# A decayed-attention and gated-MLP kernel on one core: factors of chunk 1 loaded on their own, 128-row chunk loads, a head-by-head state update, and a re-planned order

## The chip, the core and the metric

The kernel runs on one core of one Trainium2 chip. The core's engines run side by side and meet only at semaphores: PE (TensorE, matrix products into the accumulators of PSUM), DVE (VectorE) and ACT (ScalarE) for elementwise work, POOL (GpSimd), and SP (SyncE), which in this kernel issues every transfer. TensorE's clock has two levels, 1.2 and 2.4 GHz; the profile shows the granted clock as a share of the higher one. The metric is device time in microseconds (us), the median over runs.

## The reference

For 4 batches of 8 heads, 768 steps and head width 48, a state of 48x48 per head is decayed row by row and fed with an outer product; the rows that come out, 8 heads side by side, go through a gated MLP.

```python
# q, k, v, alpha: (B=4, H=8, S=768, D=48); alpha in 0.8 .. 1.0
for t in range(S):
    state = alpha[:, :, t, :, None] * state + np.einsum('bhd,bhe->bhde', k[:, :, t], v[:, :, t])
    y[:, :, t] = np.einsum('bhd,bhde->bhe', q[:, :, t], state)
x = y.transpose(0, 2, 1, 3).reshape(B * S, H * D)      # 3072 x 384
h = x @ w_in                                           # w_in 384 x 2048
g = h * np.tanh(softplus(h))
out = g @ w_out                                        # w_out 2048 x 384
```

## The kernel before

**Chunks.** Time is cut into 6 chunks of 128 steps per batch, 24 chunks in all (numbered 0 to 23; number n is batch n % 4, so chunks 0 to 3 start from an empty state). A chunk's q, k and alpha lie in one tile `qka` of 112 rows: head pairs with one head's 48 features on rows 0 to 47, the other's on rows 64 to 111. Two such tiles exist, so the load of chunk n+2 waits until chunk n has been read for the last time. `attention(n)` makes these steps:

- DVE: two running products of alpha over the chunk, backwards (`scan_rest`, L492) and forwards (`scan_front`, L509), with a small reciprocal between them (L497); the factors are multiplied into k in two halves (L504) and into q (L519); an older state is decayed (L524).
- PE: the scores (L539, 16 products recorded as 32 matmuls), DVE's causal masks (L549, two), the output of the chunk (L594; 16 products for chunks 0 to 3, with 8 more for the state part after that).
- The output goes into the tile `xs` as a rounded high part and a low part (L611, then L616 on DVE, or L623 on PE and L631 on ACT for chunks 0 to 7); six small transfers (L637) put the last two heads' rows in their places.
- For all but the last chunk of a batch: a transpose of k on PE (`turn`, L702), a copy by ACT (L706), the update `k^T v` on PE (L711: one product per head pair, 112 by 96, of which only the two 48x48 blocks on the diagonal are wanted), and its addition to the state, one DVE instruction per head of a pair (L723; for chunks 0 to 3 ACT copies, L721).

**The MLP.** A unit is one block of 128 hidden columns (16 blocks, f) over 2 or 4 chunks (256 or 512 tokens): 9 matmuls of the first layer (L754: 3 slices of 128 features, each high x high, high x low and low x high), ACT's exponential and three more activations, DVE's three steps (L772, L781, L788), and 3 matmuls of 384 columns per chunk for the second layer (L816). There are 20 units of 2 chunks, then 86 of 4. The weights come as 64-bit words; DVE makes 32-bit numbers of them (L364, L369, L374, once for each of the two matrices), ACT rounds the high part (L379), and the low part comes from PE and ACT for blocks 0 to 3 (L403, L404, L407) and from DVE for the others (L393).

**The order.** A planner in the kernel (`Plan.order`) writes all engines' instructions out in advance. Each task has an engine, a cost, a time after which its result can be used, a key, and the buffers it uses. At each step the task that can begin first is put next on its engine, the one of lower key among equals, as the planner reckons. Where PE would stand idle the planner puts in filler matmuls (L866) that write to a free accumulator and whose result is not used. Each engine then works in its order, and an instruction that waits holds up all behind it. Keys: a chunk is due some units before its first unit, spaced at least 2 units apart; weights, loads and checks hang on the same scale.

Of the kernel before, what the change touches and what calls it, by code (L numbers as in the profile page):

```python
# [9 lines left out]
F32 = mybir.dt.float32  # L10
F32R = mybir.dt.float32r
# [4 lines left out]
ALU = mybir.AluOpType  # L16
# [11 lines left out]
B, H, S, D = 4, 8, 768, 48  # L28
# [9 lines left out]
QKA = (3 * C + 1) * NPAIR + 1  # L38

# [22 lines left out]
COLD = 16  # L62
FILL_BANKS = ("o3", "o2", "o1", "o0", "h", "att")
FILL_FROM, FILL_UNTIL = 2.4, 130.0
FILL_MARGIN = 0.1
EARLY_BANKS = {
    0: "o2 h o3 o0 att att".split(),
    1: "att att att att o3 att".split(),
    2: "o0 h h h att o1".split(),
    3: "o3 h att o1 att o0".split(),  # L70
    4: "att att att att o1 h".split(),
    5: "o2 o3 att o2 o2 att".split(),
}
X_PE = 8
W_PE = 4
W_DVE = 4
# [4 lines left out]
BEGIN = {"PE": 2.4, "DVE": 4.3, "ACT": 2.2, "POOL": 4.2, "SP": 1.2}  # L81
# [17 lines left out]
class Plan:  # L99
# [23 lines left out]
    def order(self):  # L123
# [8 lines left out]
        done, n, port_free = [], len(self.tasks), 0.0  # L132

# [39 lines left out]
        while len(done) < n + fills:  # L173
            best = None
            for e in ENGINES:
                first = None
                for t in waiting[e][:WINDOW]:
# [24 lines left out]
            free[e] = at + t.cost  # L202
            if t.port:
                port_free = at + t.cost
# [14 lines left out]
WINDOW = 150  # L219

COST = {
    "load part": (0.7, 3.3), "load q": (1.8, 5.0), "load v": (0.7, 4.0), "load w": (2.0, 5.0),
    "move": (0.63, 2.5), "store": (0.47, 3.0),
    "cold fill": (0.321, 0.36), "fill": (0.1635, 0.2), "off": (0.2, 0.35), "w off": (0.95, 1.2), "lead": (0.27, 0.38), "bits": (0.47, 0.58), "w hi": (0.42, 0.56), "w lo": (0.95, 1.08),
# [3 lines left out]
    "scores": (1.07, 1.08), "y0": (1.08, 1.1), "y": (1.7, 1.7), "turn": (0.4, 0.64),  # L228
    "turned": (0.43, 0.57), "update": (0.76, 0.98),
# [14 lines left out]
def fast_path(ctx, tc, qka, v, w, out, good):  # L244
# [57 lines left out]
    xs = [const.tile([P, 2, NPAIR, k * C], F32R, name=f"xs{i}") for i, k in enumerate(X_TILES)]  # L302
# [40 lines left out]
    def weight(f):  # L343
        key = weight_unit[f] - W_LEAD
# [9 lines left out]
        got = add("SP", *COST["load w"], max(key, FIRST_W + f) - 4, load, uses=[stage])  # L354
        fs = slice(f * P, (f + 1) * P)
        for m in range(2):
# [29 lines left out]
            k = key + 0.5 * m  # L386
# [29 lines left out]
    def weight_check(f):  # L416
        key = CHECK_FROM + f * CHECK_STEP
# [30 lines left out]
    def attention(n):  # L448
# [3 lines left out]
        st, key = state[b], due[n]  # L452
# [4 lines left out]
        Q = lambda: by_pair(q_buf.tile[:, : NPAIR * C])  # L457
        K = lambda: by_pair(q_buf.tile[:, NPAIR * C : 2 * NPAIR * C])
        alpha = lambda: q_buf.tile[:, 2 * NPAIR * C :]
# [680 lines left out]
```

## Time and profile before

| | us |
|---|---|
| median of 3 runs | 523.48 (521.75 to 523.56) |
| the profiled execution | 526.62 |
| its span, first to last instruction | 524.9 |
| PE busy in the span | 513.0 (98%) |
| DVE / ACT busy | 382.3 (73%) / 397.3 (76%) |
| second layer L816 / first layer L754 on PE | 227.4 / 217.8 |

The profiled execution took 1.7 us more than its span, and 3.1 us more than the median of the runs. A busy PE is not a PE at its peak: matmuls are pipelined and their ends are modelled, so work on PE is better read from one task's start to the next one's. DVE's 73% is a mean over stages that differ: until about 143 us the weights are being made beside the first ten chunks, after that they are not.

### The profile page before, as it was taken

The page shows a single profiled execution, that of the slowest core. Times are in us where ns is not written, and L with a number is a line of the kernel's source. Part 1 is how long each engine was busy: PE and PEld are TensorE (multiplying, and loading weights), DVE is VectorE, ACT ScalarE, POOL GpSimd, SP SyncE. Part 2 cuts the span into 40 slices and gives each one's busy share as a digit, 9 for nine tenths or more (in the row PEclk, how much of TensorE's full clock was granted, in tenths as well). Part 3 has the DMA queues.
Part 4 walks back from the last instruction along what each step waited for, and adds up shares of the span by engine and source line. Part 5 has one row for each costly group of instructions (what it writes and reads, how often), then busy time and mean ns, then how long its engine had stood idle before and what let it go on. Part 6 is the DMA issues. An engine that isn't in the chain of part 4 may idle for free.

```text
span 524.9 us, 11178 instructions
## 1 busy us (share of the span) xinstructions
PE 513.0 (98%) x4287; PEld 447.7 (85%) x4287; DVE 382.3 (73%) x743; ACT 397.3 (76%) x914; POOL 4.6 (1%) x34
## 2 busy tenths in 40 slices
PE   6999999999999999899999999999999999999996
PEld 4678989998898888788899888899988899999996
DVE  6899999999976876868777566886468654554452
ACT  1578789999699987888867856577776567787774
POOL 2000000000000000000000000000000000000000
PEclk9799999999999999999999999999999999999999
DMA  8656636413254866465320132220042000010001
GB/s 269 179 172 195 200 82 205 166 61 116 68 177 139 233 229 191 169 204 162 112 76 0 47 92 76 76 76 1 1 136 78 9 9 2 15 46 1 1 1 65
DMA packets 21818, 54.31 MB, mean 103 GB/s; under 512 B 4000, under 2 KB 14752, under 8 KB 21760
## 3 DMA queue, kind: packets, MB, share of 16 engines
q1 hardware_dynamic: 21760, 53.55, 33.2%
q8 instruction: 35, 0.57, 0.5%
q14 instruction: 23, 0.19, 0.1%
HBM read 46.45 MB, written 4.72 MB: 97 GB/s over the span
## 4 chain that ended last, share of the span: by engine, by line
PE 79%; DMA 8%; DVE 7%; SPq 3%; issue 2%; ACT 2%; DVEq 0%; ACTq 0%
PE bank L816 33%; PE bank L754 32%; DMA qka<-in_qka_dram 8%; PE bank L594 5%; PE bank L539 3%; SPq L637 2%; PE bank L711 2%; PE bank L702 1%; PE bank L403 1%; DVE rest L492 1%; DVE qka L509 1%; DVE t L781 1%; DVE y L772 1%; DVE g L788 1%; DVE xs L616 1%
## 5 line engine op out<-in xcount | busy, mean ns | idle before, releaser
L816 PE MATMUL bank<-wo,g 128*128 128x384 f32 x1152 | 227.4, 341 | 0.2 <-DVE part L843 0.2
L754 PE MATMUL bank<-xs,wi 128*128 128x512 f32 (+1 forms) x954 | 217.8, 373 | 1.8 <-DVE y L772 1.8
L816 PEld LDWEIGHTS bank<-wo,g 128*128 128x128 f32 x1152 | 198.3, 188 | 7.6 <-DVE part L843 0.4
L754 PEld LDWEIGHTS bank<-xs,wi 128*128 128x128 f32 x954 | 167.4, 188 | 28.9 <-DVE y L772 2.1
L762 ACT ACTIVATE u<-bank 128x512 f32<-128x512 f32 (+1 forms) x106 | 58.9, 555 | 82.7 <-PE bank L754 82.4
L772 DVE SCALAR_TENSOR_TENSOR y<-u,bank 128x512 f32<-128x512 f32 (+1 forms) x106 | 66.8, 631 | 49.2 <-ACT u L762 48.8
L788 DVE TENSOR_TENSOR g<-t,g 128x512 fp32r<-128x512 f32 (+1 forms) x106 | 67.2, 635 | 48.0 <-ACT g L785 47.8
L775 ACT ACTIVATE t<-t,tenth 128x512 f32<-128x512 f32 (+1 forms) x106 | 72.0, 679 | 2.3
L781 DVE SCALAR_TENSOR_TENSOR t<-y,t 128x512 f32<-128x512 f32 (+1 forms) x106 | 67.0, 633 | 5.1 <-ACT t L778 4.3
L768 ACT ACTIVATE t<-u 128x512 f32<-128x512 f32 (+1 forms) x106 | 62.6, 590 | 3.7 <-DVE g L788 1.4
L785 ACT ACTIVATE g<-t 128x512 fp32r<-128x512 f32 (+1 forms) x106 | 61.5, 581 | 5.1 <-DVE t L781 3.2
L778 ACT ACTIVATE t<-t 128x512 f32<-128x512 f32 (+1 forms) x106 | 61.6, 581 | 0.5
L492 DVE TENSOR_TENSOR_SCAN rest<-qka,behind 112x516 f32<-112x516 f32 x24 | 29.5, 1228 | 15.2 <-DMA qka<-in_qka_dram 15.2
L509 DVE TENSOR_TENSOR_SCAN qka<-qka,ahead 112x516 f32<-112x516 f32 x24 | 29.4, 1223 | 0.0
L549 DVE COPY_PREDICATED probs<-causal,bank 128x384 f32<-128x384 uint32 x48 | 25.8, 584 | 4.4 <-PE bank L539 4.1
L594 PEld LDWEIGHTS bank<-probs,v 128*64 128x64 f32 (+3 forms) x768 | 20.6, 128 | 8.5 <-issue 3.9
L594 PE MATMUL bank<-probs,v 128*64 128x64 f32 (+3 forms) x768 | 25.5, 227 | 1.5 <-DVE ahead L497 1.5
L539 PEld LDWEIGHTS bank<-qka 48*64 48x64 f32 x768 | 18.6, 137 | 5.8 <-issue 3.7
L539 PE MATMUL bank<-qka 48*64 48x64 f32 (+1 forms) x768 | 22.3, 255 | 0.0
L762 ACT ACTIVATION_READ_ACCUMULATOR u<-bank 128x1 f32 x106 | 20.7, 195 | 0.0
L611 ACT ACTIVATE xs<-bank 112x256 fp32r<-112x256 f32 x48 | 16.3, 373 | 5.6 <-PE bank L594 5.6
L711 PEld LDWEIGHTS bank<-v,ks 128*112 128x112 f32 x160 | 18.0, 177 | 1.8 <-ACT xs L631 0.5
(79 smaller groups left out, 348.4 us busy)
## 6 DMA issues: line engine op xcount, KB each, us to landing
qka<-in_qka_dram SPq DMA_DIRECT2D x23, 674.2 KB, 5.5
ws<-in_wp_dram SPq DMA_DIRECT2D x16, 768.0 KB, 4.6
wc<-in_wp_dram SPq DMA_DIRECT2D x16, 768.0 KB, 5.1
v<-in_vp_dram SPq DMA_DIRECT2D x24, 192.0 KB, 4.6
out_dram<-osb SPq DMA_DIRECT2D x16, 192.0 KB, 1.8
xs<-xs SPq DMA_DIRECT2D x144, 16.0 KB, 2.5
out_dram<-part SPq DMA_DIRECT2D x8, 192.0 KB, 3.1
qka<-in_qka_dram SPq DMA_DIRECT2D x2, 224.0 KB, 3.7
```

Source lines behind the costliest of these rows:

```text
L539: nc.tensor.matmul(p[a][to, i, blocks], K()[r : r + D, j, to], q.rearrange("p (x t) -> p x t", t=HALF), start=True, stop=True,)
L594: made = nc.tensor.matmul(o, l, r, start=begins, stop=m >= len(ops) - 2, skip_group_check=True)
L754: nc.tensor.matmul(p[:, :N], wi[:, z, s, fs], x[:, a, s], start=m == 0, stop=m == len(passes) - 1)
L762: nc.scalar.activation(wide(u), wide(h), AF.Exp, scale=-1.0, accum_out=uchk[:, at : at + 1])
L768: nc.scalar.activation(wide(t), wide(u), AF.Square, bias=1.0, scale=2.0)
L772: nc.vector.scalar_tensor_tensor(wide(y), wide(u), 0.5, wide(h), ALU.add, ALU.mult)
L775: nc.scalar.activation(wide(t), wide(t), AF.Ln, bias=tenth, scale=0.1)
L778: nc.scalar.activation(wide(t), wide(t), AF.Exp, scale=-1.0)
L781: nc.vector.scalar_tensor_tensor(wide(t), wide(y), 0.4, wide(t), ALU.mult, ALU.mult)
L785: nc.scalar.activation(g.tile[:, 0, :N], wide(t), AF.Copy)
L788: late[mybir.EngineType.DVE] = nc.vector.tensor_tensor(g.tile[:, 1, :N], wide(t), g.tile[:, 0, :N].bitcast(F32), ALU.subtract)
L816: made = nc.tensor.matmul(o.tile[:, :DM], g.tile[:, a, j * C : (j + 1) * C], wo[:, z, f], start=begins and m == 0, stop=end and m == 2,)
```

## The change

Seven things change together.

- Chunk 1's tile is loaded in two parts: alpha straight after chunk 0's three parts and ahead of chunk 0's v, then q and k.
- Chunks are laid out and loaded with 128 rows in place of 112, each row starting 6656 bytes after the last (6164 before); the 16 added rows are not computed with.
- The tile `xs` holds high and low part of a chunk side by side, so a small transfer moves 16 rows of 1024 bytes in place of 16 times two runs of 512; the first layer's moving operand, which was one run of 512 columns, is now four runs of 128 with gaps of the same size.
- The update makes one product per head, with 64 or 48 columns of the array and 48 moving columns, whose results lie on the same rows as the state, so that one instruction gathers them.
- Weight block 3's low part goes from PE and ACT to DVE (`W_PE`, `W_DVE` from 4 to 3).
- The planner knows of a queue of at most 8 transfers that move one after the other, and other costs; fewer first fillers count as cold (14).
- Keys of single chunks, units and weights are shifted by a table, and the banks of the early chunks are other ones.

```diff
-COLD = 16
+COLD = 14
+SHIFT = {
+    "chunk": {
+        4: -2, 5: -2, 7: 2.79, 21: -1,
+    },
+    "unit": {
+        0: -6, 1: -4, 2: -5, 3: -3, 4: -4.5, 7: -1, 9: -1, 25: 0.5, 27: -0.9, 31: 1.5, 32: 1.01,
...
+    },
...
+}
-W_PE = 4
-W_DVE = 4
+W_PE = 3
+W_DVE = 3
...
+                    if e == "SP" and len(landed) >= QUEUE:
+                        r = max(r, landed[-QUEUE])
...
+            if e == "SP":
+                moving = max(moving, at + DMA_FIRST) + t.late
+                landed.append(moving + DMA_LAST)
+                t.late = moving + DMA_LAST - at
...
+QUEUE = 8
+DMA_FIRST, DMA_LAST = 1.67, 0.3
...
-    xs = [const.tile([P, 2, NPAIR, k * C], F32R, name=f"xs{i}") for i, k in enumerate(X_TILES)]
+    xs = [const.tile([P, NPAIR, k, 2, C], F32R, name=f"xs{i}") for i, k in enumerate(X_TILES)]
...
-            t = new(q_buf, [R, QKA], f"qka{n}")
-            nc.sync.dma_start(t, qka[b, c])
+            t = new(q_buf, [P, QKA], f"qka{n}")
+            nc.sync.dma_start(t, qka[b, c, :, :QKA])
...
+        elif n == 1:
+            got_a = add("SP", *COST["load part"], -98.7, load_part(2 * NPAIR * C, QKA), uses=[q_buf])
+            got_k = got_q = add("SP", *COST["load qk"], -98.5, load_part(0, 2 * NPAIR * C), uses=[q_buf])
...
-                    x[48 + r : 64 + r, :, s, tok].bitcast(F32),
-                    x[r + 16 * s : r + 16 * s + 16, :, NK, tok].bitcast(F32),
+                    x[48 + r : 64 + r, s, place].bitcast(F32),
+                    x[r + 16 * s : r + 16 * s + 16, NK, place].bitcast(F32),
...
-                nc.tensor.matmul(
-                    p[:R, j, : 2 * D], ks_buf.tile[:, j], V()[:, 2 * D * j : 2 * D * (j + 1)],
-                    start=True, stop=True,
-                )
+                for a, wide in ((0, HALF), (1, D)):
+                    h = (2 * j + a) * D
+                    nc.tensor.matmul(
+                        p[64 * a : 64 * a + wide, j, :D], ks_buf.tile[:, j, 64 * a : 64 * a + wide],
+                        V()[:, h : h + D], start=True, stop=True,
+                    )
...
-                    p[:, :N], wi[:, z, s, fs], x[:, a, s], start=m == 0, stop=m == len(passes) - 1
+                    p[:, :N], wi[:, z, s, fs], x[:, s, :, a], start=m == 0,
+                    stop=m == len(passes) - 1,
...
-    qka = np.zeros((B, NCH, R, QKA), inputs["q"].dtype)
+    qka = np.zeros((B, NCH, P, QKA_ROW), inputs["q"].dtype)
```

What stands on SP at the start of the program, before: chunk 0's alpha, then its k and q, chunk 0's v, then chunk 1 whole (`qka_128`), its v, weight blocks 0 and 1 (`ws`), chunk 2 (`qka_218`).

```order
L470 DMA qka_116<-in_qka_dram 112x517
L470 DMA qka_116<-in_qka_dram 112x512 x2
L474 DMA v_124<-in_vp_dram 128x384
L465 DMA qka_128<-in_qka_dram 112x1541
L474 DMA v_139<-in_vp_dram 128x384
L349 DMA ws_145<-in_wp_dram 128x1536
L349 DMA ws_179<-in_wp_dram 128x1536
L465 DMA qka_218<-in_qka_dram 112x1541
```

The same place on SP now; chunk 1's tile is `qka_120`, chunk 2's `qka_254`, and `xs` rows are the small transfers of chunk 0's output.

```order
L498 DMA qka_116<-in_qka_dram 128x517
L498 DMA qka_116<-in_qka_dram 128x512 x2
L498 DMA qka_120<-in_qka_dram 128x517
L502 DMA v_124<-in_vp_dram 128x384
L498 DMA qka_120<-in_qka_dram 128x1024
L377 DMA ws_130<-in_wp_dram 128x1536
L502 DMA v_135<-in_vp_dram 128x384
L377 DMA ws_139<-in_wp_dram 128x1536
L667 DMA xs_111<-xs_111 16x256
L493 DMA qka_254<-in_qka_dram 128x1541
```

Chunk 1's alpha is now fourth and its q and k sixth; chunk 2's load stands behind one small transfer of chunk 0's output.

What stands on DVE after chunk 1's q product (L519), before: the masks of chunk 1 (`probs`), the last step of weight block 0, and then chunk 2's backward product (L492 on `qka_218`; this listing names running products SCALAR_TENSOR_TENSOR) with block 1's steps behind it.

```order
L374 SCALAR_TENSOR_TENSOR w_lead_0_235<-ws_145,w_lead_0_235 128x384
L549 COPY_PREDICATED probs_93<-causal,bank 128x384
L549 COPY_PREDICATED probs_95<-causal,bank 128x384
L374 SCALAR_TENSOR_TENSOR w_lead_1_238<-ws_145,w_lead_1_238 128x384
L492 SCALAR_TENSOR_TENSOR rest_301<-qka_218,behind 112x516
L364 TENSOR_SCALAR w_lead_0_310<-ws_179 128x384
L497 RECIPROCAL ahead<-rest_301 112x4
```

The same place on DVE now, with chunk 2's product at L523 on `qka_254` and block 1's words in `ws_139`.

```order
L402 SCALAR_TENSOR_TENSOR w_lead_1_231<-ws_130,w_lead_1_231 128x384
L580 COPY_PREDICATED probs_93<-causal,bank 128x384
L580 COPY_PREDICATED probs_95<-causal,bank 128x384
L392 TENSOR_SCALAR w_lead_0_304<-ws_139 128x384
L397 SCALAR_TENSOR_TENSOR w_lead_0_304<-ws_139,w_lead_0_304 128x384
L402 SCALAR_TENSOR_TENSOR w_lead_0_304<-ws_139,w_lead_0_304 128x384
L392 TENSOR_SCALAR w_lead_1_321<-ws_139 128x384
L523 SCALAR_TENSOR_TENSOR rest_327<-qka_254,behind 112x516
```

Weight block 0 is finished before chunk 1's masks, and four steps of block 1 now stand ahead of chunk 2's backward product.

What stands on PE for chunk 1's update now (before, one row, `L711 MATMUL bank<-v_139,ks_262 112x96 x4`), with the low part of weight block 1 (L431, L432) ahead of it and the first of 13 fillers behind it.

```order
L431 MATMUL bank<-w_lead_0_304,ident 128x384
L432 MATMUL bank<-wi,minus_ident 128x384
L743 MATMUL bank<-v_135,ks_283 64x48
L743 MATMUL bank<-v_135,ks_283 48x48
L743 MATMUL bank<-v_135,ks_283 64x48
L743 MATMUL bank<-v_135,ks_283 48x48
L743 MATMUL bank<-v_135,ks_283 64x48
L743 MATMUL bank<-v_135,ks_283 48x48
L743 MATMUL bank<-v_135,ks_283 64x48
L743 MATMUL bank<-v_135,ks_283 48x48
L895 LDWEIGHTS behind
L895 MATMUL bank<-behind 128x384
```

Four products of 96 moving columns have become eight of 48. Over the whole of PE's order there are now 50 fillers (43 before), 6 pairs of weight subtractions L431 and L432 (8 before), and the first unit's first layer stands after chunk 2's output and ahead of chunk 3's scores (before: behind chunk 3's scores).

## Rows read from the trace of the kernel before

**Rows 1.** The page: busy us, share of the span, instructions of each engine.

```profile
PE 513.0 (98%) x4287; PEld 447.7 (85%) x4287; DVE 382.3 (73%) x743; ACT 397.3 (76%) x914; POOL 4.6 (1%) x34
```

**Rows 2.** Windows: stretch, length, busy us (instructions) per engine, PE clock, DMA share, GB/s.

```profile
117.00:130.00 13.00, 13.00 (x84) 11.60 (x87) 13.00 (x29) 12.00 (x27) 0.00 (x0) 1.00 0.27 79
...
208.00:260.00 52.00, 49.90 (x464) 42.47 (x463) 38.96 (x72) 45.37 (x103) 0.26 (x3) 1.00 0.54 170
```

**Rows 3.** Finer windows of the start, the same columns.

```profile
2.50:7.50 5.00, 4.92 (x18) 2.49 (x19) 3.88 (x8) 0.46 (x2) 0.99 (x5) 1.00 1.01 281
...
19.00:20.00 1.00, 1.00 (x4) 0.68 (x3) 0.87 (x1) 0.28 (x1) 0.00 (x0) 0.50 0.13 31
```

**Rows 4.** Timeline of the start: start, busy, engine, line, tiles, shapes, [idle before <-releaser].

```profile
9.93 1.23 DVE L492 TENSOR_TENSOR_SCAN rest<-qka,behind 112x516 f32<-112x516 f32 x1 [2.23 <-DMA qka<-in_qka_dram]
11.08 1.02 DVE L549 COPY_PREDICATED probs<-causal,bank 128x384 f32<-128x384 uint32 x2
...
12.15 1.06 PE L594 MATMUL bank<-probs,v 128*64 128x64 f32 x32 [1.53 <-DVE ahead L497]
...
20.70 1.06 PE L594 MATMUL bank<-probs,v 128*64 128x64 f32 x32
...
24.98 0.90 PE L539 MATMUL bank<-qka 48*64 48x128 f32 x32
```

**Rows 5.** DMA issues from 0 to 4.2 us: count, KB each, median us to landing.

```profile
qka<-in_qka_dram SPq DMA_DIRECT2D x1, 674.2 KB, 7.2
```

**Rows 6.** Timeline of DVE, 26 to 47 us.

```profile
35.15 1.22 DVE L492 TENSOR_TENSOR_SCAN rest<-qka,behind 112x516 f32<-112x516 f32 x1
...
39.20 0.35 DVE L524 TENSOR_TENSOR state<-state,rest 112x192 f32<-112x192 f32 x1
...
40.44 0.62 DVE L364 TENSOR_SCALAR w_lead<-ws 128x384 int32<-128x384 int32 x2
...
42.85 1.05 DVE L549 COPY_PREDICATED probs<-causal,bank 128x384 f32<-128x384 uint32 x2
43.80 0.41 DVE L781 SCALAR_TENSOR_TENSOR t<-y,t 128x256 f32<-128x256 f32 x1
```

**Rows 7.** Timeline of PE, 26 to 47 us.

```profile
30.93 0.81 PE L403 MATMUL bank<-w_lead,ident 128*128 128x384 f32 x2
...
31.84 0.90 PE L539 MATMUL bank<-qka 48*64 48x128 f32 x32
...
39.70 0.90 PE L539 MATMUL bank<-qka 48*64 48x128 f32 x32
...
44.46 0.66 PE L594 MATMUL bank<-qka,state 48*48 48x128 f32 x16
```

**Rows 8.** Timeline of PE at a state update, 174 to 179 us.

```profile
176.69 0.93 PE L711 MATMUL bank<-v,ks 128*112 128x96 f32 x8
177.40 1.29 PE L816 MATMUL bank<-wo,g 128*128 128x384 f32 x6
```

**Rows 9.** Windows of L594 alone, PE and weight loads: middle part of a chunk's output.

```profile
302.82:303.43 0.61, 0.61 (x20) 0.54 (x16) 1.00 0.01 3
```

**Rows 10.** Groups by line and form: xcount | busy us, mean ns | idle before.

```profile
L723 DVE TENSOR_TENSOR state<-bank,state 48x192 f32<-48x192 f32 x32 | 11.3, 352 | 5.9 <-PE bank L711 5.7
```

**Rows 11.** The chain that ended last: start us, us, what.

```profile
85.72 1.08 PE bank L754 x9
...
109.36 2.08 PE bank L754 x9
111.43 2.08 PE bank L816 x12
```

**Rows 12.** Who waited for whom, DVE, 143 to 330 us: total us, times, longest.

```profile
DVE rest L492 <- DMA qka<-in_qka_dram: 11.8, 9, 3.6
```

**Rows 13.** The page: DMA issues over the span, median us to landing.

```profile
qka<-in_qka_dram SPq DMA_DIRECT2D x23, 674.2 KB, 5.5
ws<-in_wp_dram SPq DMA_DIRECT2D x16, 768.0 KB, 4.6
```

More of the change, by code (lines that the diff above doesn't have):

```diff
@@ L219 @@
 WINDOW = 150
+QUEUE = 8
+DMA_FIRST, DMA_LAST = 1.67, 0.3
 COST = {
-    "load part": (0.7, 3.3), "load q": (1.8, 5.0), "load v": (0.7, 4.0), "load w": (2.0, 5.0),
-    "move": (0.63, 2.5), "store": (0.47, 3.0),
-    "cold fill": (0.321, 0.36), "fill": (0.1635, 0.2), "off": (0.2, 0.35), "w off": (0.95, 1.2), "lead": (0.27, 0.38), "bits": (0.47, 0.58), "w hi": (0.42, 0.56), "w lo": (0.95, 1.08),
+    "load part": (0.47, 1.1), "load qk": (0.47, 1.8), "load q": (0.47, 2.7),
+    "load v": (0.47, 0.82), "load w": (0.45, 2.51), "move": (0.6, 0.15), "store": (0.47, 0.75),
+    "cold fill": (0.321, 0.36), "fill": (0.1635, 0.2), "off": (0.125, 0.3), "w off": (0.95, 1.2), "lead": (0.27, 0.38), "bits": (0.47, 0.58), "w hi": (0.42, 0.56), "w lo": (0.95, 1.08),
     "w check": (0.92, 1.2),
@@ L227 @@
     "state": (0.365, 0.4), "state0": (0.31, 0.35), "mask": (0.49, 0.63),
-    "scores": (1.07, 1.08), "y0": (1.08, 1.1), "y": (1.7, 1.7), "turn": (0.4, 0.64),
-    "turned": (0.43, 0.57), "update": (0.76, 0.98),
+    "scores": (1.02, 1.05), "y0": (1.1, 1.2), "y": (1.77, 1.79), "turn": (0.42, 0.64),
+    "turned": (0.43, 0.57), "update": (0.7, 0.9),
     "x hi": (0.275, 0.415), "x lo": (0.34, 0.455),
@@ L343, in weight @@
     def weight(f):
-        key = weight_unit[f] - W_LEAD
+        key, shift = weight_unit[f] - W_LEAD, SHIFT["weight"].get(f, 0.0)
         stage = plan.buffer("stage")
@@ L463, in load @@
         def load():
-            t = new(q_buf, [R, QKA], f"qka{n}")
-            nc.sync.dma_start(t, qka[b, c])
+            t = new(q_buf, [P, QKA], f"qka{n}")
+            nc.sync.dma_start(t, qka[b, c, :, :QKA])
         def load_part(lo, hi):
             def part():
-                t = q_buf.tile if q_buf.tile is not None else new(q_buf, [R, QKA], f"qka{n}")
+                t = q_buf.tile if q_buf.tile is not None else new(q_buf, [P, QKA], f"qka{n}")
                 nc.sync.dma_start(t[:, lo:hi], qka[b, c, :, lo:hi])
@@ L731, in attention @@
                 *(("ACT", *COST["state0"]) if first else ("DVE", *COST["state"])), key + 1.0,
-                gather(a, r), [t_u, t_y, *t_decay], [u_buf],
+                gather, [t_u, t_y, *t_decay], [u_buf],
             )
-            for a, r in enumerate((0, 64))
         ]
@@ L740, in unit @@
     def unit(c0, nt, f, at, ends):
-        N, key = nt * C, float(at)
+        N, key = nt * C, at + SHIFT["unit"].get(at, 0.0)
         tile_at, place = X_AT[c0]
-        x = xs[tile_at][:, :, :, place * C : place * C + N]
+        x = xs[tile_at][:, :, place : place + nt]
         fs = slice(f * P, (f + 1) * P)
```

64 lines of the change are left out of this document (35 added, 29 removed), and 2 rows, old and new, of the table SHIFT.

## The prediction

> **What bounds the kernel now.** I read the page first: PE is busy 98% of the span, DVE 73% [rows 1]. Then windows. From 30 us on PE hardly stands still: at 117 to 130 us it is busy all 13.00 us, and so is DVE [rows 2], so for the first ten chunks two engines are full at once. The steady pace is 2.08 us for a first layer of 512 columns and 2.08 for its 12 second-layer matmuls, start to start [rows 11], and 86 such units (with 20 of half the size) make some 400 us that the change leaves alone. Time can come only from work taken off PE, from the start, where PE runs fillers and waits for DVE, and from the idle 2.1 us (52.00 less 49.90) between 208 and 260 us [rows 2].
>
> At the start the chain goes through DVE. DVE waits 2.23 us until chunk 1's load lands and begins its backward product at 9.93; behind it the masks of chunk 0 come at 11.08 and PE's first output at 12.15, after 1.53 us with nothing to do [rows 4]. The granted clock then is at 0.50, the 1.2 GHz level, at 19 to 20 us [rows 3], and chunk 1's output, which stands behind weight block 0 on PE, comes at 20.70 [rows 4]. The first products of the MLP follow chunk 3's scores at 31.84 [rows 7].
>
> **Part by part.** All sums are made against the profiled execution, 526.62 us (span 524.9 and 1.7 around it). It lies 3.1 above the median of 523.48; I apply the same difference to the median.
>
> *Chunk 1's alpha first.* It is fourth in the queue: 1.05 MB with what stands ahead. At the 281 GB/s of 2.5 to 7.5 us [rows 3] that is 3.7 us of transfer, so it lands at about 6 us if transfers go strictly in order, and no later than 8 if those behind take a share (chunk 1's whole tile took 7.2 us from issue [rows 5]). I take 7.9, near the moment at which DVE is through with chunk 0. That takes 2.0 us off the wait, and its cover is gone at once: from there DVE is late by its own work. I follow it in the new order with start-to-start times: a chunk's backward and forward products and its three multiplications 3.7 us (35.15 to 39.20, less one unit step of 0.3), the six steps of a weight block 2.4 (40.44 to 42.85), two masks 0.95 (42.85 to 43.80) [rows 6]; the first product of a chunk is 1.2 of the 3.7.
>
> - product of chunk 1 at 7.9, masks of chunk 0 to 10.1: output 0 at 10.1 (before 12.15).
> - rest of chunk 1's factors 2.5, weight block 0 2.4, masks 0.95: output 1 at 16.0 (before 20.70).
> - four steps of block 1, 1.5. Chunk 2's load now stands behind the transposes of chunk 1, at about 13; with 5.5 us [rows 13] it lands at 18.7, and DVE waits 1.2 us for it, a new wait. Factors 3.7 and one weight step 0.5: scores of chunk 2 at 22.9 (before 24.98).
> - one weight step, product of chunk 3, masks: 25.5; rest of its factors 2.5: scores of chunk 3 at 28.0 (before 31.84).
> - three weight or unit steps and masks, 2.8; five small ones, 2.0; chunk 4's factors with two unit steps 4.3: scores of chunk 4 at 37.1 (before 39.70). Seven more steps, 3.0: output 4 at 40.2 (before 44.46).
>
> The lead is 4.3 us at output 4. DVE never strings its work together so tightly, and q and k of chunk 1 land with 1.78 MB, a little late; I take 3.5, with 1.0 (the alpha alone, half given back to the new wait) and 5.0 as ends. At that point PE also has more behind it: six second-layer matmuls more, 1.04 [rows 11], and one weight subtraction more, 0.9 (30.93 to 31.84 [rows 7]), but chunk 4's transposes and update not yet, 1.1 (the update 0.71 [rows 8], the transposes put at half of it). That is 0.9 in its favour: 4.4.
>
> *Update by heads.* Before, 0.71 us from the update's start to the next task (176.69 to 177.40 [rows 8]). After, eight products of 48 columns, two at a time on halves of the array. The nearest row is the middle part of a chunk's output: eight products of 64 columns with the same 128 rows and the same halves, 0.61 us with the change-over to that part (16 weight loads, two to a product) [rows 9]. By columns that is 0.46, by count of products 0.61; whether the 0.15 between them is a change-over or a price per product no row tells. I take 0.5, so 0.2 saved. The ends are 0 (the price per product and a change-over of 0.1 to 0.15 more) and 0.3. For chunks 4 to 19, where PE is full, 16 times 0.2 is 3.2; the four early updates lie beside DVE's chain and bring nothing.
>
> The section Key Properties of the Trainium skill's page "TensorEngine Tiling (Array Packing)" speaks against this part: a change of tiling mode drains the engine, and the update now enters and leaves a mode of half-width tiles. The trace has that 0.15 at one such change and does not contradict the rule; with two drains of that size and 0.46 between them the update would cost 0.76, and the sum would lose the 3.2 us.
>
> *Gather, weight block 3.* One gather replaces two: 16 of 0.35 us less on DVE [rows 10], of which the four of chunks 4 to 7 help while DVE is full. Block 3 moves two subtractions of 0.5 to DVE and takes two pairs of 0.9 off PE, already in the count above. Counting the rows of both orders up to unit 20's last step on DVE, at the means of their groups, gives 110.6 us before and 108.1 after: DVE has 2.5 less to do there, so it can carry a lead of 3.5 plus 2 to 143 us. PE's lead by then is 4.4 and six updates, 1.2. The two agree; nothing is lost, but nothing is to spare.
>
> *128-row loads, wide small transfers.* A chunk's load takes 5.5 us for 674 KB, a weight block's, on 128 rows, 4.6 for 768 [rows 13]. If the chunk's comes to that pace it lands 0.8 earlier. DVE waits 11.8 us for chunk loads between 143 and 330, nine times [rows 12]; PE has work in store during nearly all of it, and the 2.1 us idle are what is left of it. Ends: 2.6 better, 2 worse (a load placed too late stops everything behind it on DVE). I take 0.6 better. The small transfers move the same bytes; nothing waits for their last microsecond, so 0.
>
> *Fillers.* 50 in place of 43; as before 43 stand ahead of the first unit, in DVE's shadow. Two of the seven later ones come after output 4: 0.3.
>
> **Sum:** 4.4 + 3.2 + 0.6 - 0.3 = 7.9 us; 526.6 becomes 518.7, and the median 523.5 becomes 515.5 (rounded).
>
> **Rivals.**
> - *The update saves nothing* (each new change-over costs about 0.15). For it: 0.61 where 0.46 would do by columns [rows 9]. Against: the update of before, 112 columns wide, is no part of the steady pace either and has its own change-overs, which the 0.71 holds [rows 8]. Then 523.5 - 4.7 = 518.8.
> - *DVE takes the lead back.* It is as full as PE at 117 to 130 us [rows 2]; if the shifted keys put weight steps ahead of what PE waits for, PE idles and only what DVE has less to do comes through, 2 to 2.5, with 0.6 to 1 of late updates: 520.9, on the edge of no change.
> - *More than forecast:* the idle of 182 to 260 us goes whole (2 more), the early chain holds at 4.3 and the update at 0.3: 523.5 - 12 = 511.5. For it: nine long waits for loads with a planner that now reckons with the queue.
> - *Slower: the first layer reads x in four runs with gaps.* No row shows PE streaming with gaps. A matmul of 512 columns takes 231 ns (2.08 / 9), one of 256 takes 120 (1.08 / 9) [rows 11], so a break costs 9 ns if it acts like a new matmul. Three breaks in 774 matmuls and one in 180 are 22.5 us: 523.5 - 7.9 + 22.5 = 538. Spread over the same breaks, the 7.9 us gained are 3 ns each: from there it decides. No row speaks against it either; it gets little because each break would have to cost about a third of a new matmul's start only to cancel the gain.
>
> **How the numbers follow.** Forecast as summed, within 512.5 and 518: 0.52. Update saves nothing: 0.15. DVE takes it back: 0.15. More than forecast: 0.14. Slower by the gaps: 0.04. A measurement here can tell some 0.5%, 2.6 us, from no change: faster is under 520.9, slower over 526.1. Forecast, first and third rival are all faster (0.81), of the second a third (0.05): 0.86; the rest of it is no change, 0.10; slower 0.04. The range of 8 in 10 runs from 510, half of the third rival in, to 521, the edge of the second.
>
> **What would show it.** Chunk 1's product without a wait of 2 us, at about 8; outputs 0, 1 and 4 near 10, 16 and 41 us, and a granted clock that stays at 2.4 GHz between 13 and 20 us, or drops later; an update of 0.5 us to the next start; first layers of 512 columns still at 2.08; fewer than 11.8 us of DVE waiting for chunk loads after 143. I am wrong if outputs 1 and 4 keep their times, if 2.08 grows, or if PE shows idle time between 40 and 143 us.

## The result and the profile after

The changed kernel takes 516.8 us (median of 4, 516.63 to 517.6) where the kernel before, timed beside it, takes 523.52 (median of 4): a ratio of 0.9868, with the interval 0.9832 to 0.9904. It is faster, by 6.7 us; I had said 515.5 and a range of 510 to 521. The profiled execution took 516.63 us, with a span of 514.9. Against the profiled execution of before (span 524.9) that is 10.0 us, more than between the medians, since that one lay 3.1 above its median.

The page: busy times as in [rows 1], the DMA queue of the loads (packets, MB, share of 16 engines) and the loads as in [rows 13].

```profile
PE 506.9 (98%) x4448; PEld 439.7 (85%) x4448; DVE 377.4 (73%) x729; ACT 393.6 (76%) x908; POOL 4.6 (1%) x34
...
q1 hardware_dynamic: 20016, 55.91, 31.3%
...
qka<-in_qka_dram SPq DMA_DIRECT2D x22, 770.5 KB, 4.6
ws<-in_wp_dram SPq DMA_DIRECT2D x16, 768.0 KB, 4.3
```

PE's busy time is 6.1 us shorter although it issues 161 matmuls more. Part of the 6.1 is the half clock in the profiled execution of before, at which the same work counts as longer: b_xs (below), which has the order of before and no fall of the clock at the start, shows 510.7 busy. A chunk's load moves 14% more bytes and lands 0.9 us sooner than in [rows 13]; it now has the pace of a weight block.

The start in the timeline, columns as in [rows 4]: chunk 1's product, outputs 0 and 1, chunk 2's product, the scores of chunks 2 and 4, and the first part of output 4.

```profile
7.62 1.23 DVE L523 TENSOR_TENSOR_SCAN rest<-qka,behind 112x516 f32<-112x516 f32 x1
...
10.12 1.06 PE L625 MATMUL bank<-probs,v 128*64 128x64 f32 x32
...
15.94 1.06 PE L625 MATMUL bank<-probs,v 128*64 128x64 f32 x32
...
18.68 1.23 DVE L523 TENSOR_TENSOR_SCAN rest<-qka,behind 112x516 f32<-112x516 f32 x1 [0.44 <-DMA qka<-in_qka_dram]
...
22.92 0.90 PE L570 MATMUL bank<-qka 48*64 48x128 f32 x32 [0.43 <-issue]
...
37.05 0.90 PE L570 MATMUL bank<-qka 48*64 48x128 f32 x32
...
39.80 0.66 PE L625 MATMUL bank<-qka,state 48*48 48x128 f32 x16
```

Chunk 1's product starts with no wait where [rows 4] has 2.23 us; output 1 is 4.8 us earlier, output 4 (44.46 in [rows 7]) 4.66.

Windows: two stretches of [rows 2] and [rows 3] again, and all of 143 to 330 us.

```profile
19.00:20.00 1.00, 1.00 (x18) 0.58 (x16) 1.00 (x2) 0.37 (x2) 0.00 (x0) 1.00 0.62 101
...
143.00:330.00 187.00, 187.00 (x1757) 160.29 (x1756) 134.81 (x245) 154.26 (x347) 0.88 (x10) 1.00 0.41 140
...
208.00:260.00 52.00, 52.00 (x588) 44.28 (x587) 38.73 (x72) 44.53 (x102) 0.35 (x4) 1.00 0.47 167
```

The clock is at its upper level, 2.4 GHz, at 19 to 20 us (0.50 in [rows 3]), and PE's idle time at 208 to 260 us is gone. Of the 2.1 us that it was before, part differs from execution to execution: b_xs, in the old order, has 51.44 us busy of these 52.00. Who waited, DVE, 143 to 330 us, against 11.8 us and nine times in [rows 12]:

```profile
DVE rest L523 <- DMA qka<-in_qka_dram: 3.3, 4, 1.5
```

An update with the first layer ahead of it, the six second-layer matmuls behind it and the start of the next task. First before, around the two lines of [rows 8], then the changed kernel:

```profile
174.64 2.20 PE L754 MATMUL bank<-xs,wi 128*128 128x512 f32 x9
...
178.62 0.90 PE L539 MATMUL bank<-qka 48*64 48x128 f32 x32
```

```profile
220.35 2.20 PE L782 MATMUL bank<-xs,wi 128*128 128x512 f32 x9
222.49 0.67 PE L743 MATMUL bank<-v,ks 128*64 128x48 f32 x16
223.08 1.31 PE L845 MATMUL bank<-wo,g 128*128 128x384 f32 x6
224.32 0.90 PE L570 MATMUL bank<-qka 48*64 48x128 f32 x32
```

From its own start to the next one an update now takes 0.60 us (0.71 before). But the first layer ahead of it takes 2.14 to the update's start where it took 2.05, and the matmuls behind it 1.24 where they took 1.22. From the first to the last of the four starts it is 3.97 us, and 3.98 before: here the update by heads saves PE 0.01 us.

Two pieces of the chain as in [rows 11]:

```profile
101.90 2.08 PE bank L845 x12
...
139.57 4.12 PE bank L782 x18
```

A first layer of 512 columns with no update behind it takes 2.06 to 2.08 as before: reading x with gaps costs nothing.

Where the 10 us between the two profiled executions came from can be counted on PE, since it hardly stands still: the time from each of its instructions to the next, summed by kind of task (a wait, and what a task costs the matmul ahead of it, counts with the one ahead). The update gives 3.0 (14.9 to 11.9), the second layer 3.1 (212.8 to 209.7, most of it the waits between 182 and 260 us), subtractions on PE 2.3 (8.1 to 5.7), transposes 1.3, scores 0.8, fillers 0.4; the first layer is 1.1 longer. The update's 3.0 is therefore no gain of that size: what it costs its neighbours stands under the first and the second layer.

### The profile page after: what moved, and what is told of

Read it like the earlier page. It is cut to its first block, busy times and chain, and to the rows that moved or that the text cites. A ratio compares the mean times of both kernels' runs of the same rounds, so it can differ in the third digit from the quotient of the medians.

```text
span 514.9 us, 11417 instructions
## 1 busy us (share of the span) xinstructions
PE 506.9 (98%) x4448; PEld 439.7 (85%) x4448; DVE 377.4 (73%) x729; ACT 393.6 (76%) x908; POOL 4.6 (1%) x34
## 3 DMA queue, kind: packets, MB, share of 16 engines
q1 hardware_dynamic: 20016, 55.91, 31.3%
## 4 chain that ended last, share of the span: by engine, by line
PE 94%; DVE 3%; DMA 1%; ACT 0%; issue 0%; DVEq 0%
PE bank L845 40%; PE bank L782 39%; PE bank L625 6%; PE bank L570 3%; PE bank L743 2%; PE bank L732 1%; PE bank L895 1%; DMA qka<-in_qka_dram 1%; DVE probs L580 1%; DVE rest L523 0%; DVE qka L540 0%; PE bank L653 0%; DVE w_lead L397 0%; PE bank L431 0%; DVE qka L550 0%
## 5 line engine op out<-in xcount | busy, mean ns | idle before, releaser
L845 PE MATMUL bank<-wo,g 128*128 128x384 f32 x1152 | 224.2, 341 | 0.0
L797 ACT ACTIVATE t<-u 128x512 f32<-128x512 f32 (+1 forms) x106 | 62.5, 590 | 10.1 <-DVE g L817 8.6
L523 DVE TENSOR_TENSOR_SCAN rest<-qka,behind 112x516 f32<-112x516 f32 x24 | 29.4, 1226 | 4.6 <-DMA qka<-in_qka_dram 4.4
L535 DVE TENSOR_TENSOR qka<-qka,rest 112x256 f32<-112x256 f32 x48 | 19.2, 401 | 0.0
```

Of the source, the lines that this page charges most:

```text
L797: nc.scalar.activation(wide(t), wide(u), AF.Square, bias=1.0, scale=2.0)
L845: made = nc.tensor.matmul(o.tile[:, :DM], g.tile[:, a, j * C : (j + 1) * C], wo[:, z, f], start=begins and m == 0, stop=end and m == 2,)
```

## The experiments

All twelve were timed in three groups, each beside the kernel before on one chip (medians 524.68, 523.68 and 523.57 us). Those that begin with a_ start from the changed kernel, those with b_ from the one before. The ratios on record are not quotients of two medians; where the two measures tell different sizes, both are given.

**The changed kernel again.**

> The changed kernel once more, as the measure for its three variants on the same chip. 516.8 us, ratio to before 0.987; the profile should again show no wait for chunk 1's alpha and no stretch at half clock.

517.45 us, ratio 0.9846 (0.9811 to 0.9882): the result repeats.

**The alpha's place: a_swap** lets chunk 1's q and k go first; nothing else moves.

```diff
-got_a = add("SP", *COST["load part"], -98.7, load_part(2 * NPAIR * C, QKA), uses=[q_buf])
-got_k = got_q = add("SP", *COST["load qk"], -98.5, load_part(0, 2 * NPAIR * C), uses=[q_buf])
+got_a = add("SP", *COST["load part"], -98.7, load_part(0, 2 * NPAIR * C), uses=[q_buf])
+got_k = got_q = add("SP", *COST["load qk"], -98.5, load_part(2 * NPAIR * C, QKA), uses=[q_buf])
```

> The changed kernel with the places of chunk 1's two part loads exchanged: q and k fourth, alpha sixth; the order of all other instructions is the same. Theory 1 (the start goes through DVE, and DVE stays full until 143 us): alpha lands at about 9.3 in place of 6.5, chunk 1's product begins at 9.3 in place of 7.6, and the 1.7 us stay until the end: 518.5; if the longer idle of PE before output 0 also brings a stretch at the 1.2 GHz level, up to 521. Rival (PE's fillers take it up and the lead does not count): 516.8 to 517.3.

518.70 us, 1.25 above the run again beside it (executions 518.27 to 519.78 against 516.69 to 518.81; the two intervals against before overlap). Timeline of a_swap:

```profile
8.89 1.23 DVE L523 TENSOR_TENSOR_SCAN rest<-qka,behind 112x516 f32<-112x516 f32 x1 [1.19 <-DMA qka<-in_qka_dram]
...
11.12 1.06 PE L625 MATMUL bank<-probs,v 128*64 128x64 f32 x32 [0.50 <-DVE ahead L528]
...
16.93 1.06 PE L625 MATMUL bank<-probs,v 128*64 128x64 f32 x32
```

Outputs 0 and 1 are 1.0 later than in the changed kernel's timeline, output 8 still is (126.20 against 125.23), and about that much is there at the end: in this order, time lost at the start was not made up.

**The same from the other side: b_alpha**, the kernel before with chunk 1's load in two parts, alpha first.

```diff
-            nc.sync.dma_start(t, qka[b, c])
+            a = 2 * NPAIR * C
+            for lo, hi in ((a, QKA), (0, a)) if n == 1 else ((0, QKA),):
+                nc.sync.dma_start(t[:, lo:hi], qka[b, c, :, lo:hi])
```

> The kernel before, with chunk 1's one load issued as two at the same place: alpha, then q and k. Every other instruction is as before. Theory 1 (the wait for chunk 1's alpha, and the stretch at 1.2 GHz that follows PE's idle time, hold up DVE and so everything until 143 us): chunk 1's product at about 8 in place of 9.93, output 0 at 10.3, no stretch at half clock or a shorter one: 2 to 4 us less, 519.5 to 521.5. Rival (PE was already full afterwards, so the order has to be made anew to use an earlier start): 523.0 to 523.5.

523.25 us, ratio 0.9969 (0.9947 to 0.9991): some 1.6 us off before by the ratio and 0.4 by the medians, short of the 2 to 4 of theory 1, though output 1 is 4.2 us earlier than in [rows 4]. Its timeline shows where the lead ends:

```profile
7.87 1.23 DVE L494 TENSOR_TENSOR_SCAN rest<-qka,behind 112x516 f32<-112x516 f32 x1 [0.17 <-DMA qka<-in_qka_dram]
...
16.51 1.06 PE L596 MATMUL bank<-probs,v 128*64 128x64 f32 x32
...
18.21 1.23 DVE L494 TENSOR_TENSOR_SCAN rest<-qka,behind 112x516 f32<-112x516 f32 x1 [1.99 <-DMA qka<-in_qka_dram]
```

DVE comes earlier to chunk 2's product and waits 1.99 us for that chunk's load. The wait is moved from chunk 1 to chunk 2. What the early alpha does to the clock is told under b_fill.

**The half clock: b_fill**, nine fillers more ahead of output 0.

```diff
-            nc.tensor.matmul(
+            for _ in range(10 if i == 21 else 1):
+                nc.tensor.matmul(
```

> The kernel before, with nine more fillers on PE ahead of output 0, where PE stands idle for 1.5 us; nothing else. Theory 1 (the idle time there lets the granted clock fall to 1.2 GHz from 13.7 to 20.5 us, and that costs PE 2 to 2.5 us of slow work): the clock stays at 2.4 GHz, output 1 comes some 2 us earlier than at 20.7, and the kernel is 1 to 2.5 us faster: 521 to 522.5. Rival A (the clock falls all the same): 523.5. Rival B (the clock stays, but DVE sets the pace there): clock 0.998, time within 0.5 of before.

524.42 us, ratio 0.9994 (0.9969 to 1.0019). A window of b_fill, and then the same of before:

```profile
13.00:21.00 8.00, 7.93 (x122) 5.34 (x117) 8.00 (x16) 5.14 (x15) 0.00 (x0) 1.00 0.58 134
```

```profile
13.00:21.00 8.00, 7.96 (x76) 4.87 (x68) 6.53 (x15) 3.94 (x11) 0.00 (x0) 0.57 0.45 108
```

The clock is up in b_fill. DVE, busy 6.53 us of the 8.00 before, is now busy all of them. The fall is not in every execution of the old order either. The same stretch of b_xs (below; its order is that of before) and of its output 0 in PE's timeline:

```profile
13.00:21.00 8.00, 7.82 (x107) 4.99 (x107) 8.00 (x17) 5.63 (x16) 0.00 (x0) 1.00 0.57 122
```

```profile
12.27 1.06 PE L594 MATMUL bank<-probs,v 128*64 128x64 f32 x32 [0.74 <-DVE probs L549]
```

PE waited 0.74 us there, not 1.53, and the clock stayed up; its outputs 1 to 8 come 2 to 2.7 us before those of the profiled execution of before. About that much of the 10.0 us may lie between executions of one kernel, and the medians' 6.7 are the better measure of the change.

How often the clock falls can be told from the mean granted clock of every timed execution. Of the 60 of before that were timed beside these runs, 21 had 0.985 to 0.995, with a median of 526.1 us, and 39 had 0.996 to 1.00, with 523.3. I take the lower group to be those with the fall: the two profiled executions with so low a mean, before (0.991) and b_update (0.992), both show 0.57 at 13 to 21 us. The fall then costs some 2.8 us where it comes. So low a mean was found in 3 of 12 executions of b_xs and 6 of 12 of b_update, in none of b_fill (12) and b_alpha (12), and in none of the other kernels.

So the fillers do keep the clock up. b_fill's median is 1.7 below the executions of before on its chip with the low clock (526.1) and 1.1 above those without (523.3): its ratio near 1 is a sum of a gain in some executions and a cost in the others, and its output 0 comes 0.5 us later than that of b_xs (12.76 against 12.27). The early alpha prevents the fall too. Beside the executions of before whose clock stayed up, b_alpha's 523.25 is 0.1 us off; what it gains in the ratio is, as far as these numbers go, the fall that it spares.

**The update: a_pair**, the changed kernel with the products by pairs and two gathers, **and b_update**, the kernel before with products by heads and one gather. The edit of b_update (that of a_pair is its reverse):

```diff
-                nc.tensor.matmul(
-                    p[:R, j, : 2 * D], ks_buf.tile[:, j], V()[:, 2 * D * j : 2 * D * (j + 1)],
-                    start=True, stop=True,
-                )
+                for a, wide in ((0, HALF), (1, D)):
+                    h = (2 * j + a) * D
+                    nc.tensor.matmul(
+                        p[64 * a : 64 * a + wide, j, :D], ks_buf.tile[:, j, 64 * a : 64 * a + wide],
+                        V()[:, h : h + D], start=True, stop=True,
+                    )
```

> The changed kernel with the update by pairs of heads and two gathers, as before, in the same places. Theory 1 (the update by heads is worth what the traces show, 0.71 to 0.59 us, sixteen times where PE is full): 1.9 us more, and up to 2.5 with the four early ones: 518.7 to 519.3. Rival (its price is hidden or given back): 516.8. A second rival, that DVE's second gathers are what counts before 143 us, adds 4 x 0.3 to the 1.9 there: 520.

> The kernel before, with the update by heads and one gather in the place of the first of the two; all other instructions in the order of before. Theory 1: 16 x 0.12 = 1.9 less, and up to 2.5: 521.0 to 521.6. Rival (the order of before stalls on DVE and chunk loads at 182 to 260 us, and the time saved on PE turns into longer stalls there): 522.5 to 523.5, with more than 2.6 us of idle PE between 182 and 260 us.

a_pair: 519.56 us, 2.1 above the run again. b_update: 523.06 us, ratio 0.9977 (0.9953 to 1.0), some 1.2 off before by the ratio and 0.6 by the medians; theory 1's 521.0 to 521.6 is missed.

On PE neither run shows a saving of that size. a_pair has the same tasks around an update as the changed kernel above, and they too take 3.97 us:

```profile
222.27 2.20 PE L782 MATMUL bank<-xs,wi 128*128 128x512 f32 x9
...
226.24 0.90 PE L570 MATMUL bank<-qka 48*64 48x128 f32 x32
```

Counted with the matmul ahead and the one behind, the sixteen updates of chunks 4 to 19 take 18.6 and 18.7 us by pairs in b_xs and b_loads and 18.4 by heads in b_parts, and 18.7 by pairs in a_pair and 18.2 by heads in the changed kernel. Up to output 4 a_pair is 0.3 behind the changed kernel (40.12 against 39.80), at output 8 it is 1.2 (126.40 against 125.23), in the stretch in which DVE is full; that fits the second rival, DVE's second gathers, but no run changed the gather alone. In b_update the first update's saving goes into a longer wait of PE ahead of output 0 (1.53 in [rows 4]):

```profile
PE bank L594 <- DVE ahead L497: 2.2, 1, 2.2
```

The rival's longer stalls at 182 to 260 us are not there: PE is idle for 0.8 us in that stretch of b_update's profile, and for 2.6 in that of before.

**The loads: a_112**, the changed kernel with 112 rows again, **a_128u**, with 128 rows at the old row length, **and b_loads**, the kernel before with 128 rows alone. Core of the edits of a_112 and of a_128u (only in the array that is loaded from), and of b_loads:

```diff
-            nc.sync.dma_start(t, qka[b, c, :, :QKA])
+            nc.sync.dma_start(t[:R], qka[b, c, :, :QKA])
...
-    qka = np.zeros((B, NCH, P, QKA_ROW), inputs["q"].dtype)
+    qka = np.zeros((B, NCH, R, QKA), inputs["q"].dtype)
```

```diff
-    qka = np.zeros((B, NCH, P, QKA_ROW), inputs["q"].dtype)
+    qka = np.zeros((B, NCH, P, QKA), inputs["q"].dtype)
```

```diff
-            t = new(q_buf, [R, QKA], f"qka{n}")
-            nc.sync.dma_start(t, qka[b, c])
+            t = new(q_buf, [P, QKA], f"qka{n}")
+            nc.sync.dma_start(t, qka[b, c, :, :QKA])
```

> The changed kernel with chunks laid out and loaded with 112 rows of 6164 bytes, as before; the order is the same. Theory 1: loads take 5.5 us again in place of 4.6, DVE waits for them 10 us or more in place of 4.4, PE has work in store for most of it: 517 to 518.5. Rival A (the loads removed the stalls of 182 to 260 us): 519.5, with PE idle 2 us there. Rival B (the order alone removed them): 516.8, no idle.

> The changed kernel with 128 rows that lie 6164 bytes apart in memory, as the 112 rows did before, in place of 6656; same order. Theory 1 (the row count decides: 128 rows spread over the transfer engines as the weights' loads do): packets of 6164 bytes at about 290 ns as in the changed kernel, loads 4.7 us, time 517 to 518. Rival (the start of each row decides: 6656 is a multiple of 512, 6164 is not): packets at 350 ns, loads over 5.5 us for 14% more bytes, 521 or more.

> The kernel before with 128-row loads of chunks alone (rows 6656 bytes apart); order and all else as before. Known so far: all parts in the order of before give 0.986, alpha first alone 0.997, the update alone 0.998. Theory 1 (the rest is the loads: DVE's in-order wait for them falls from 15 us to about 6, and with it PE's stalls at 182 to 260 us): 519 to 520.5, ratio 0.992. Rival A (no part is worth much alone, they work only together): 522 or more. Rival B (the small transfers or the layout of x make the rest): 523, and the run with that alone shows it.

a_112: 520.94 us, ratio 0.9921 (0.9892 to 0.9951), 3.5 above the run again and above what any of its three theories gave. a_128u: 517.79 us, 0.9889 (0.9868 to 0.991), 1.0 above the changed kernel's 516.8 and 0.3 above the run again. b_loads: 519.48 us, 0.9921 (0.9902 to 0.9939), 4.1 off before (3.7 off those executions of before on its chip whose clock stayed up, 523.2) and the largest of the single parts. Of a_112, in four fences: the page's rows on DMA, the place in PE's timeline, DVE's waits over the span, and a window:

```profile
q1 hardware_dynamic: 19584, 53.55, 33.2%
...
qka<-in_qka_dram SPq DMA_DIRECT2D x22, 674.2 KB, 5.2
```

```profile
193.82 0.60 PE L732 MATMUL bank<-ident,qka 112*128 112x112 f32 x4 [1.80 <-DVE xs L646]
194.20 1.98 PE L845 MATMUL bank<-wo,g 128*128 128x384 f32 x6
```

```profile
DVE rest L523 <- DMA qka<-in_qka_dram: 12.2, 10, 3.5
```

```profile
194.00:198.00 4.00, 4.00 (x29) 3.47 (x29) 3.51 (x7) 4.00 (x11) 0.00 (x0) 0.57 0.10 28
```

The loads are later, DVE waits 12.2 us for them over the span (4.7 in the run again), what stands behind them on DVE is late once by 1.80 us for PE, and the clock then falls to near its lower level, 1.2 GHz, for some 4 us, which costs about 1.7 more (4.00 times the 0.43 that is missing). The start loses as well. Output 4 in a_112, and then in the run again:

```profile
40.75 0.66 PE L625 MATMUL bank<-qka,state 48*48 48x128 f32 x16
```

```profile
39.20 0.66 PE L625 MATMUL bank<-qka,state 48*48 48x128 f32 x16
```

Start (1.55), stall and clock come to about 5.0 us, where the span, 519.8, is 3.6 above that of the run again, 516.2, which itself lost 0.9 us of PE's time between 143 and 260 us. The fall at 194 us belongs to this execution; the eight others of a_112, at a mean clock of 0.997 to 1.00, have a median of 520.8 all the same. So the 3.5 between the medians does not rest on it, and how they divide over start and stalls is not shown. Of a_128u and b_loads the loads:

```profile
qka<-in_qka_dram SPq DMA_DIRECT2D x22, 770.5 KB, 4.7
```

```profile
q1 hardware_dynamic: 22176, 55.91, 32.0%
...
qka<-in_qka_dram SPq DMA_DIRECT2D x23, 770.5 KB, 4.7
```

Both have 128 rows, one with each distance between rows (6164 and 6656 bytes), and the same 4.7 us: the count of rows decides, not where a row starts. b_loads at the start, timeline:

```profile
8.66 1.23 DVE L493 TENSOR_TENSOR_SCAN rest<-qka,behind 112x516 f32<-112x516 f32 x1 [0.96 <-DMA qka<-in_qka_dram]
...
16.53 1.23 DVE L493 TENSOR_TENSOR_SCAN rest<-qka,behind 112x516 f32<-112x516 f32 x1
16.68 1.06 PE L595 MATMUL bank<-probs,v 128*64 128x64 f32 x32
```

Chunk 1's whole tile lets DVE begin 1.27 us earlier (9.93 in [rows 4]), and chunk 2's is there before DVE asks for it. So the wider load alone takes half of the wait that the early alpha was made for, and it spares the wait for chunk 2 that b_alpha has.

**x with gaps: b_xs**, the kernel before with the new layout of x and the small transfers of 1024 bytes.

```diff
-    xs = [const.tile([P, 2, NPAIR, k * C], F32R, name=f"xs{i}") for i, k in enumerate(X_TILES)]
+    xs = [const.tile([P, NPAIR, k, 2, C], F32R, name=f"xs{i}") for i, k in enumerate(X_TILES)]
...
-                    p[:, :N], wi[:, z, s, fs], x[:, a, s], start=m == 0, stop=m == len(passes) - 1
+                    p[:, :N], wi[:, z, s, fs], x[:, s, :, a], start=m == 0, stop=m == len(passes) - 1
```

> The kernel before with high and low part of x side by side: small transfers of 16 runs of 1024 bytes, first layer's moving operand in four runs with gaps; order and all else as before. Theory 1: nothing waits for the last part of a small transfer and a gap costs nothing: 523 to 524, first layers at 2.08 us. Rival (half the packets free the transfer engines for the chunk loads): 521 to 522, chunk loads under 5.3 us.

523.22 us, ratio 0.999 (0.9967 to 1.0012): nothing. The first layer in the groups by line of b_xs, and then of before:

```profile
L753 PE MATMUL bank<-xs,wi 128*128 128x512 f32 (+1 forms) x954 | 217.8, 373 | 0.9 <-DVE y L771 0.9
```

```profile
L754 PE MATMUL bank<-xs,wi 128*128 128x512 f32 (+1 forms) x954 | 217.8, 373 | 1.8 <-DVE y L772 1.8
```

**The order: b_parts**, the order and planner of before with the four edits together (alpha first, update by heads, 128-row loads, x layout), **and b_parts_w3**, the same with weight block 3 on DVE.

```diff
-W_PE = 4
-W_DVE = 4
+W_PE = 3
+W_DVE = 3
```

> The kernel before with all the changed parts but weight block 3 and the order: chunk 1's alpha ahead of its q and k at the place of its one load, 128-row loads, small transfers of 1024 bytes, update by heads with one gather; all in the order of before. Theory 1: 2 to 3 from the start, 1.9 from the update, 0.5 to 1 from the loads: 518 to 519.5. Rival (the new order is what makes the difference): 522 or more. A second rival, that the strided moving operand costs something, shows as first layers over 2.08 us.

> All changed parts with weight block 3's low part on DVE, and an order made by the planner of before, with its costs, keys and banks: the kernel that leaves out only the new planner and its shifts. Theory 1 (block 3 takes two pairs of 0.9 off PE and the order matters little): 515.5 to 516.5. Rival (DVE, full until 143 us, or an order that its shifts no longer suit takes it back): 517 to 519, with more than 12 us of fillers on PE.

b_parts: 517.09 us, ratio 0.9858 (0.9822 to 0.9894), better than either theory and not to be told from the changed kernel. b_parts_w3: 518.13 us, 0.9892 (0.987 to 0.9915), 1.0 above b_parts, its interval overlapping. Groups of PE, b_parts and then b_parts_w3 (fillers, subtractions):

```profile
L871 PE MATMUL bank<-behind 112*128 112x384 bf16 x43 | 10.2, 383 | 2.6 <-DVE behind L284 2.6
L404 PE MATMUL bank<-w_lead,ident 128*128 128x384 f32 x16 | 6.9, 512 | 0.0
```

```profile
L871 PE MATMUL bank<-behind 112*128 112x384 bf16 x54 | 12.7, 379 | 2.6 <-DVE behind L284 2.6
L404 PE MATMUL bank<-w_lead,ident 128*128 128x384 f32 x12 | 5.2, 512 | 0.0
```

What block 3 takes off PE comes back as fillers. That this is because DVE, which now does it, is the engine that PE waits for at the start is likely, but not shown by itself: the planner made a new order for this run.

The start of a chunk's output on PE (us) in the profiled executions puts the parts beside each other. b_xs stands for before without the fall of the clock:

| output | before | b_xs | b_alpha | b_loads | b_parts | after |
|---|---|---|---|---|---|---|
| 1 | 20.70 | 18.00 | 16.51 | 16.68 | 15.75 | 15.94 |
| 2 | 27.75 | 25.05 | 24.85 | 23.73 | 22.26 | 25.61 |
| 4 | 44.46 | 42.50 | 41.98 | 40.42 | 39.06 | 39.80 |
| 8 | 133.21 | 131.25 | 130.72 | 129.22 | 127.65 | 125.23 |
| 19 | 339.81 | 335.21 | 336.76 | 332.62 | 329.73 | 333.59 |

Against b_xs the early alpha leads by 1.5 at output 1, by 0.2 at output 2 and by 0.5 at output 4; the loads by 1.3 and 1.3, and by 2.1 at output 4; all parts together by 2.3, 2.8 and 3.4; the changed kernel at output 4 by 2.7. (Outputs 8 and 19 of after stand at another place in its order.)

## Why the prediction was right, and where its parts were off

*What bounds the kernel.* Right: PE is full in both, and the early chain goes through DVE. The claim that PE shows no idle time between 40 and 143 us held.

*Chunk 1's alpha and the chain at the start.* The alpha landed at 6.53 us (taken 7.9, with 6 to 8 as ends), and the rest came as followed by hand: output 0 at 10.12 (10.1), output 1 at 15.94 (16.0), scores 2, 3 and 4 at 22.92, 28.13 and 37.05 (22.9, 28.0, 37.1), output 4 at 39.80 (40.2). The new wait for chunk 2's load is there with 0.44 us (1.2). "DVE never strings its work together so tightly" was wrong: the hand chain held. Two other steps failed. The lead was counted from 44.46, in an execution with the half clock, and then taken off a median, 523.5, that is hardly above the 523.3 of the executions without it ("I apply the same difference to the median"). Against b_xs, whose clock stayed up, the changed kernel leads by 2.7 at output 4, where the sum has 3.5 and, with what stands behind, 4.4. And the sum books the whole lead to the early alpha. Taken out of the changed kernel the alpha costs 1.25; alone it brings 0.4 (medians) to 1.6 (ratio), and 0.1 beside those executions of before whose clock stayed up. At least as much of the lead comes with the wider loads: 2.1 of the 3.4 at output 4 in b_parts, and a_112 is 1.0 behind the changed kernel there and 1.6 behind the run again.

*Loads.* The term that was furthest too small: "I take 0.6". Alone the 128 rows bring 3.7 to 4.1, and without them the changed kernel loses 3.5. The pace was right (0.9 earlier, 0.8 said), but I set it only against the waits after 143 us. The same 0.8 stands at the start too, at chunk 1's and chunk 2's tiles, where PE has no work in store. And I took the slack of PE after 143 us for granted: the profiled execution of a_112 has a stall of 1.80 us there and the clock behind it. The end that I gave, 2.6 better, was too narrow for that.

The section on Door 1 of the Trainium skill's page "SBUF — State Buffer" says that a transfer's bandwidth follows the number of ports that its partitions reach, and by its table 112 partitions from 0 on reach all 16. By that alone 112 rows should cost no more than their bytes. The runs differ: 53.55 MB take 33.2% of the engines' time with 112 rows, 55.91 MB take 32.0% with 128 at the same row length. The advice of this page of the Trainium skill, to use 128 partitions, holds here.

*Update by heads.* This mechanism was wrong. The update's own time fell from 0.71 to 0.60 us, where I said 0.5, but I read [rows 8] from the update's start on and so left out the matmul ahead of it. That one takes 0.09 longer to the update's start, the next one 0.02, and 0.11 less 0.11 leaves nothing: 3.97 us for the whole stretch in place of 3.98, and 0.2 to 0.5 us over sixteen updates in place of 3.2. The rule that a change of tiling mode drains the engine (the Trainium skill, "TensorEngine Tiling (Array Packing)", Key Properties), which I had quoted against this part, agrees with that: the 0.09 stands where the update's mode is entered. So the rival "the update saves nothing" is right for PE, at change-overs smaller than its 0.15. a_pair and b_update still show 2.1 and 0.6 to 1.2 for products and gather together; the one gather in place of two (16 of 0.35 us on DVE) is what is left to explain them, and that is not shown.

*Weight block 3, gather, order.* The 0.9 of the sum that stood for more work behind output 4 does not show by itself: the old order with the four other parts is as fast. Fillers took 12.3 us in the changed kernel and 9.9 in b_parts, which takes back the 1.7 to 1.8 that block 3 saves on PE. The 0.3 that I took for fillers counts only the two behind output 4.

*x with gaps and small transfers.* Right: 0, shown by b_xs, whose first layers take 202.6 us in all from start to start, as in before. The slower rival is excluded.

*DVE takes the lead back.* Not in the changed kernel. In b_alpha a load takes it back, and in b_update PE waits 0.7 longer for DVE ahead of output 0.

So the total, 6.7 against 7.9, is right for the path (less wait at the start, fewer stalls behind loads) and not for its shares, and that it came so near is partly luck: a start counted from an execution with half clock and an update whose saving PE does not show were too large by about what the loads were too small. The four parts alone add to 5.5 us by the medians (0.43, 0.62, 4.09 and 0.35), where b_parts has 6.6; their ratios multiply to 0.9858, just that of b_parts, but each is known to 0.002 only. The three taken out of the changed kernel add to 1.25 + 2.1 + 3.5 = 6.9 us.

What stays open: why a load on 112 rows is slower for its bytes; what one gather is worth without the change of the products; and what the new order does apart from block 3, which no run took by itself.

## What to carry to other kernels

A shorter transfer counts at every place where an engine stands in order behind it, the start above all: look for all its waits, not for those of one stretch, and ask of a lead which of the parts of a change would each bring it alone. A load moved forward often moves the wait to the load behind it. When two engines are full at once, work taken from one and given to the other can come back as fillers or waits in the first, as with weight block 3 here. A task's price includes what the instruction ahead of it pays: compare a stretch that begins before the task and ends after it. And before a difference that is read from one profiled execution is taken off a median, see whether that execution is like most of them.

## What the runs showed of the hardware that I had not expected

- A load of 112 rows of 6164 bytes holds the DMA engines longer than one of 128 such rows: 5.2 against 4.7 us to landing (a_112 and a_128u), 33.2% against 32.0% of their time in all.
- Entering a stretch of half-width products cost the matmul ahead of it 0.09 us (2.14 against 2.05 to the update's start) and leaving it 0.02: all that the update had saved by its own time.
- The same kernel on the same chip ran with or without a fall of the clock: 21 of 60 executions of before at a mean of 0.985 to 0.995, 2.8 us longer than the others.
- A stall of PE of 1.80 us was followed by 4 us at a mean granted clock of 0.57 (a_112), and one of 1.53 by 0.57 from 13 to 21 us (before); one of 0.74 in b_xs was followed by no fall. The length of the stall alone does not decide: before has one of 1.79 at 1.00 all through 208 to 260 us [rows 2].

```profile
212.48 2.34 PE L754 MATMUL bank<-xs,wi 128*128 128x512 f32 x9 [1.79 <-DVE y L772]
```

- Reading x in four runs with gaps costs PE nothing that 954 matmuls would show: 373 ns of one in both layouts.
